# Every step of an attention-plus-MLP kernel listed one by one, with a new order for its first two batches

## The chip, the cores and the metric

The kernel runs on one core of a Trainium2 chip. The metric is the device time of one execution in microseconds (us). The engines are named as in the profile: PE (TensorE), DVE (VectorE), ACT (ScalarE), POOL (GpSimd) and SP (SyncE, which issues all transfers here); PEld is PE's weight loading. A measurement of this kernel tells about 0.3% from no change.

## What is computed

Eight batches of 8 heads, 576 tokens, head width 64, with 32 packed queries `p` per head; then a feed-forward layer over all 4608 tokens, 512 wide inside the model and 2048 wide in the middle:

```python
def sm_attn(qq, kk, vv):
    s = scale * np.matmul(qq, kk.transpose(0, 1, 3, 2))
    s = s - np.max(s, axis=-1, keepdims=True)
    a = np.exp(s)
    a = a / (np.sum(a, axis=-1, keepdims=True) + 1e-09)
    return np.matmul(a, vv)
p_packed = sm_attn(p, k, v)
out = sm_attn(q, p_packed, p_packed)
x = out.transpose(0, 2, 1, 3).reshape(B * S, H * D)
h = x @ w_in
g = h * (1.0 / (1.0 + np.exp(-1.702 * h)))
result = g @ w_out
```

## The kernel before

Inputs come as float32, except that the two weight matrices come as 64-bit floats, which the kernel turns into float32 itself. A weight piece is 128 rows of 512 numbers; there are 32, in `queue`: per chunk c of the 2048 middle columns four pieces of `w_in` ("in") and four of `w_out` ("out"). Piece n takes these steps: `load_w` (SP), `begin_w` (ACT: exponent scaled), `shift_w`, `sign_w`, `low_w` (DVE). An "out" piece is then split in a rounded upper part (`upper_w`, ACT) and the rest (`lower_w`, DVE, or two products on PE and an ACT copy for pieces 4 and 5). Raw pieces lie in 16 buffers that "in" and "out" pieces of a chunk share, so an "out" piece can be loaded only when an "in" piece has gone through `low_w`.

Attention of batch b, first pass: `scores1` (PE, in two halves of 288 tokens), maxima (DVE, `mx`), exponentials (ACT, `exp1`), `turn1` (transposes on PE, copies on ACT), `pack` (PE), `pack_end` (ACT), `pack_turn` (PE, then ACT): this gives `PT`. `m_chunk` multiplies `PT` with a chunk of `w_in`, so that the second attention pass and the first product of the feed-forward layer become one; its result is split in `mhi` (ACT) and `mlo` (DVE, `m_lower`). Second pass, per half: `scores2` (PE), `scores2_turn`, maximum and `sub2` (DVE), `exp2` (ACT), `sum2`, normalising and a transpose to `xt` (DVE), then a split in `ahi` (ACT) and `alo` (POOL, or PE and ACT in batch 0).

The feed-forward layer works in units (b, f): f is one of 16 pieces of 128 middle columns. `unit_h` gives six products `h` per half (upper and lower parts), tanh (ACT, `g`), the gate (DVE, `g` and, for the last 64 tokens, `over`), and a split in `ghi` (ACT) and `glo` (POOL). `unit_out` adds 3 products for each of four blocks of 128 tokens into `acc0` to `acc3`. The 64 tokens of a batch that are left over are done for two batches at once (`acc_over`). Batches 0 and 1 are interleaved, since weights are still being made: batch 0 chunk 0, batch 1 chunks 0 and 1, batch 0 chunks 1 to 3, batch 1 chunks 2 and 3; unfinished sums go to memory (`aside`) and come back (`back`).

Order: PE and SP execute in the order of the code. For DVE, ACT and POOL a scheduler with a model of times chose the order. The code is a hand-written list `lead` up to the first units, then a plan per unit. `warm(n)` is n products without use, which keep PE busy. The functions that the change touches:

Of the kernel before, what the change touches and what calls it, by code (L numbers as in the profile page):

```python
# [18 lines left out]
def kernel(  # L19
# [34 lines left out]
    P = 128  # L54
# [68 lines left out]
    def load(what, b, halves=(0, 1)):  # L123
        if what == "p":
            t = wk.tile([P, NP, NPK], F32, tag="p_sb", name=f"p_{b}", bufs=2)
            nc.sync.dma_start(t, pT[b])
            kq["p", b] = t
            return
# [8 lines left out]
        if what == "v":  # L137
            nc.sync.dma_start(
                t[:, : KC - 1, :], v[b, : (KC - 1) * P, :].rearrange("(c p) e -> p c e", p=P)
            )  # L140
            nc.sync.dma_start(t[:KLAST, KC - 1, :], v[b, (KC - 1) * P :, :])
        else:
            src = kT if what == "k" else qT
            for half in halves:
                nc.sync.dma_start(t[:, :, tokens(half)], src[b, :, :, tokens(half)])
# [50 lines left out]
    def low_w(n):  # L196

# [7 lines left out]
        if w[0] == "in" and w[1] > 0:  # L205
            load_w(("out", i))
# [10 lines left out]
    def lower_w_pe(n, bank):  # L217

        w = wo[slot_of(queue[n])]
        bank = bank(f"pswl_{n}")  # L220
        nc.tensor.matmul(bank, ident, dec[n], start=True, stop=False)
        nc.tensor.matmul(bank, minus, w[:, 0, :], start=False, stop=True)
        nc.scalar.copy(w[:, 1, :], bank)

    def make_w(*ns):


        for step in (begin_w, shift_w, sign_w, low_w):
# [26 lines left out]
    def scores1_first(eo, half):  # L255
# [7 lines left out]
        for j in range(NP):  # L263
            mm1(0, eo, half, bank, j)
        nc.vector.tensor_reduce(
            st["mx", 1, 0, eo][:, half : half + 1], bank[:, :NH], axis=AX.X, op=ALU.max
        )
        st["bank", eo, half] = bank

    def scores1(b, half):  # L270
# [3 lines left out]
        banks = [bank_b(f"ps1_{b}_{eo}_{half}") for eo in range(2)]  # L274
# [3 lines left out]
        for eo in range(2):  # L278
            nc.scalar.copy(st["x", 1, b, eo][:, tokens(half)], banks[eo][:, :NH])
            nc.vector.tensor_reduce(  # L280
                st["mx", 1, b, eo][:, half : half + 1], banks[eo][:, :NH], axis=AX.X, op=ALU.max
            )

    def exp1(b, eo):
        key = (1, b, eo)
        mx, x = st["mx", *key], st["x", *key]
        nb = wk.tile([P, 1], F32, tag="nb1", name=f"nb1_{b}_{eo}", bufs=2)
        st["sum", *key] = sm = wk.tile([P, 2], F32, tag="sm1", name=f"sm1_{b}_{eo}", bufs=2)
        nc.vector.tensor_scalar(nb, mx[:, 0:1], mx[:, 1:2], -SCALE, op0=ALU.max, op1=ALU.mult)
        if b > 0:  # L290
            nc.scalar.activation(x, x, AF.Exp, bias=nb, scale=SCALE, accum_out=sm[:, 0:1])
            return
        for half in range(2):
            nc.scalar.activation(
                x[:, tokens(half)], st["bank", eo, half][:, :NH], AF.Exp, bias=nb,
                scale=SCALE, accum_out=sm[:, half : half + 1],
            )
# [58 lines left out]
    def pack_turn(b):  # L356
        bank = bank_b(f"pspt_{b}")
        nc.tensor.transpose(bank[:, :P], st["P", b].rearrange("p e d -> p (e d)"), ident)
        st["PT", b] = PT = wk.tile([P, NP, NPK], F32, tag="PT", name=f"PT_{b}", bufs=3)
        nc.scalar.copy(PT.rearrange("p j n -> p (j n)"), bank[:, :P])  # L360

    def m_chunk(b, fc):

        PT = st["PT", b]
        banks = [bank_b(f"psm_{b}_{fc}_{eo}") for eo in range(2)]
        for j in range(NP):
            for eo in range(2):
# [6 lines left out]
                )  # L374
        for eo in range(2):
            hi = wk.tile([P, FC], F32R, tag=f"mhi{eo}", name=f"mhi_{b}_{fc}_{eo}", bufs=2)
            nc.scalar.copy(hi, banks[eo])  # L377
            st["m", b, fc, eo] = [hi, banks[eo]]

    def m_lower(b, fc):  # L380
        for eo in range(2):
            hi, bank = m = st["m", b, fc, eo]
            m[1] = wk.tile([P, FC], F32R, tag=f"mlo{eo}", name=f"mlo_{b}_{fc}_{eo}", bufs=2)
            nc.vector.tensor_tensor(m[1], bank, hi.bitcast(F32), op=ALU.subtract)  # L384
# [21 lines left out]
    def scores2_turn(b, half):  # L406
        x = st["x", 2, b, half]
        for eo, bank in enumerate(st["bank", 2, b, half]):
            nc.vector.transpose(x[:, eo * NH : (eo + 1) * NH], bank[:, :NH])
# [30 lines left out]
    def norm2(b, half):  # L440
        key = (2, b, half)
        x, rs = st["x", *key], st["rs", *key]
        st["t", *key] = t = x_tile(f"xt_{b}_{half}")
        nc.vector.tensor_tensor(groups(x), groups(x), over(rs), op=ALU.mult)
        nc.vector.transpose(t, x)
# [8 lines left out]
    def a_lower_pe(b, half, banks):  # L454
# [282 lines left out]
```

## Time and profile before

| | |
|---|---|
| time, median of 3 | 750.83 us (749.62 to 751.96) |
| profiled execution: time, span | 750.82 us, 748.7 us |
| mean granted clock of PE | 0.983 |
| busy: PE, DVE, ACT, POOL | 716.1, 345.9, 338.4, 239.3 us |
| moved by DMA | 60.08 MB, mean 80 GB/s |

Busy is the sum of the time in which an engine had an instruction in work. A list by stretches of time says in which stage an engine is full. In the chain of work that ended last each piece is followed back to what released it. A row of the timeline gives start, length, engine, line and, in brackets, the idle time before it and who ended it.

### The profile page before, as it was taken

The page shows a single profiled execution, that of the slowest core. Times are in us where ns is not written, and L with a number is a line of the kernel's source. Part 1 is how long each engine was busy: PE and PEld are TensorE (multiplying, and loading weights), DVE is VectorE, ACT ScalarE, POOL GpSimd, SP SyncE. Part 2 cuts the span into 40 slices and gives each one's busy share as a digit, 9 for nine tenths or more (in the row PEclk, how much of TensorE's full clock was granted, in tenths as well). Part 3 has the DMA queues.
Part 4 walks back from the last instruction along what each step waited for, and adds up shares of the span by engine and source line. Part 5 has one row for each costly group of instructions (what it writes and reads, how often), then busy time and mean ns, then how long its engine had stood idle before and what let it go on. Part 6 is the DMA issues. An engine that isn't in the chain of part 4 may idle for free.

```text
span 748.7 us, 13113 instructions
## 1 busy us (share of the span) xinstructions
PE 716.1 (96%) x5084; PEld 569.6 (76%) x5084; DVE 345.9 (46%) x808; ACT 338.4 (45%) x813; POOL 239.3 (32%) x292
## 2 busy tenths in 40 slices
PE   5687989999999999999999999999999999999997
PEld 4455877678877877878877888878887887888886
DVE  3789499953283227232274217243255226432220
ACT  3473566654344444353435434454335444443331
POOL 0022343343352324333343333423334323433332
PEclk7799999999999999999999999999999999999999
DMA  9750743640423021030213022021113100010002
GB/s 296 252 177 1 282 168 113 222 141 28 154 69 121 12 65 65 1 123 1 64 64 120 18 65 64 1 73 52 51 63 121 29 1 2 1 57 1 1 1 70
DMA packets 35133, 60.08 MB, mean 80 GB/s; under 512 B 2304, under 2 KB 19712, under 8 KB 35072
## 3 DMA queue, kind: packets, MB, share of 16 engines
q1 hardware_dynamic: 35072, 59.25, 23.8%
q8 instruction: 40, 0.66, 0.4%
q14 instruction: 21, 0.17, 0.1%
HBM read 47.71 MB, written 11.53 MB: 79 GB/s over the span
## 4 chain that ended last, share of the span: by engine, by line
PE 84%; DVE 10%; DMA 2%; ACT 1%; issue 1%; POOL 0%; SPq 0%; ACTq 0%; DVEq 0%
PE acc L528 43%; PE h L504 25%; PE acc_over L528 6%; PE psm L368 4%; DVE dec L191 2%; DMA raw<-w_in 2%; PE pspv L341 2%; PE ps L397 1%; PE ps L243 1%; DVE g L494 1%; DVE dec L187 1%; PE pst L317 1%; DVE dec L201 1%; DVE mlo L384 1%; DVE w_in L201 1%
## 5 line engine op out<-in xcount | busy, mean ns | idle before, releaser
L491 POOL TENSOR_TENSOR glo<-g,ghi 128x224 fp32r<-128x224 f32 (+1 forms) x256 | 198.2, 791 | 459.1 <-ACT ghi L490 458.6
L528 PE MATMUL acc<-wo,ghi 128*128 128x512 f32 x1024 | 320.9, 395 | 0.5 <-ACT ghi L490 0.5
L528 PEld LDWEIGHTS acc<-wo,ghi 128*128 128x128 f32 x1024 | 186.5, 189 | 36.7 <-ACT ghi_over L490 2.5
L494 DVE SCALAR_TENSOR_TENSOR g<-g,h 128x224 f32<-128x224 f32 (+1 forms) x256 | 105.5, 418 | 225.9 <-ACT g L509 225.3
L528 PE MATMUL acc<-wo,glo 128*128 128x512 f32 x512 | 201.9, 394 | 0.0
L509 ACT ACTIVATE g<-h 128x288 f32<-128x288 f32 x256 | 104.5, 411 | 161.2 <-PE h L504 157.0
L504 PE MATMUL h<-ahi,mhi 128*128 128x288 f32 x512 | 151.6, 311 | 6.5 <-DVE g L494 4.5
L504 PE MATMUL h<-ahi,mlo 128*128 128x288 f32 x512 | 144.3, 297 | 1.9 <-DVE mlo L384 1.8
L504 PEld LDWEIGHTS h<-ahi,mhi 128*128 128x128 f32 x512 | 96.6, 189 | 46.3 <-issue 28.8
L528 PEld LDWEIGHTS acc<-wo,glo 128*128 128x128 f32 x512 | 96.7, 189 | 22.9 <-POOL glo L491 0.6
L490 ACT CAST ghi<-g 128x224 fp32r<-128x224 f32 (+1 forms) x256 | 100.3, 402 | 23.7 <-DVE g L494 12.6
L504 PE MATMUL h<-alo,mhi 128*128 128x288 f32 x512 | 108.4, 293 | 0.0
L504 PEld LDWEIGHTS h<-ahi,mlo 128*128 128x128 f32 x512 | 96.8, 189 | 4.4 <-DVE mlo L384 2.3
L504 PEld LDWEIGHTS h<-alo,mhi 128*128 128x128 f32 x512 | 82.7, 188 | 0.0
L384 DVE TENSOR_TENSOR mlo<-psm,mhi 128x512 fp32r<-128x512 f32 x64 | 41.4, 685 | 74.6 <-ACT mhi L377 74.6
L377 ACT CAST mhi<-psm 128x512 fp32r<-128x512 f32 x64 | 34.3, 588 | 52.5 <-PE psm L368 52.5
L528 PE MATMUL acc_over<-wo,ghi_over 128*128 128x512 f32 x128 | 40.1, 395 | 0.5 <-ACT ghi_over L490 0.5
L368 PE MATMUL psm<-w_in,PT 64*32 64x512 f32 x512 | 36.9, 601 | 2.0 <-DVE w_in L201 2.0
L183 ACT ACTIVATE dec<-raw 128x512 f32<-128x512 f32 x32 | 21.4, 674 | 16.3 <-DMA raw<-w_in 9.0
L528 PEld LDWEIGHTS acc_over<-wo,ghi_over 128*128 128x128 f32 x128 | 23.4, 188 | 6.8 <-ACT ghi_over L490 1.4
L466 POOL TENSOR_TENSOR alo<-xt,ahi 128x576 fp32r<-128x576 f32 x14 | 20.0, 1429 | 23.1 <-ACT ahi L451 19.1
L494 DVE SCALAR_TENSOR_TENSOR over<-g,h 128x64 f32<-128x64 f32 x128 | 27.3, 213 | 0.0
(73 smaller groups left out, 482.1 us busy)
## 6 DMA issues: line engine op xcount, KB each, us to landing
k<-kT SPq DMA_DIRECT2D x16, 576.0 KB, 5.2
q<-qT SPq DMA_DIRECT2D x16, 576.0 KB, 5.4
raw<-w_in SPq DMA_DIRECT2D x16, 512.0 KB, 8.0
v<-v SPq DMA_DIRECT2D x8, 1024.0 KB, 5.8
raw<-w_out SPq DMA_DIRECT2D x16, 512.0 KB, 5.3
o<-o SPq DMA_DIRECT2D x24, 256.0 KB, 2.1
aside<-o SPq DMA_DIRECT2D x8, 256.0 KB, 2.1
back<-aside SPq DMA_DIRECT2D x8, 256.0 KB, 6.3
```

The source lines that it names most:

```text
L183: nc.scalar.activation(dec[n], upper, AF.Abs, scale=DOWN)
L191: nc.vector.scalar_tensor_tensor(t, raw[slot_of(queue[n])][:, :, 1], 0x80000000, t, op0=ALU.bitwise_and, op1=ALU.bitwise_or,)
L368: nc.tensor.matmul(banks[eo][32 * j : 32 * j + 32, :], PT[rows(eo), j, :], w_in_sb[fc][rows(eo), j, :], start=True, stop=True,)
L377: nc.scalar.copy(hi, banks[eo])
L384: nc.vector.tensor_tensor(m[1], bank, hi.bitcast(F32), op=ALU.subtract)
L466: nc.gpsimd.tensor_tensor(lo, st["t", 2, b, half], hi.bitcast(F32), op=ALU.subtract)
L490: nc.scalar.copy(hi, src)
L491: nc.gpsimd.tensor_tensor(lo, src, hi.bitcast(F32), op=ALU.subtract)
L494: nc.vector.scalar_tensor_tensor(dst, th, 1.0, h, op0=ALU.add, op1=ALU.mult)
L504: nc.tensor.matmul(h[:, :NH], m[eo][part][:, fo : fo + P], a[:, eo * NH : (eo + 1) * NH], start=(n == 0), stop=(n == len(terms) - 1),)
L509: nc.scalar.activation(g, h[:, :NH], AF.Tanh, scale=1.702)
L528: nc.tensor.matmul(acc, gp[:, at : at + P], wo[f][:, part, :], start=(start and i == 0), stop=(stop and i == 2),)
```

## The change

1. Every step that used two engines is split in functions for one engine each: for instance `scores1` into `scores1_mm` (PE), `scores1_copy` (ACT) and `scores1_max` (DVE), `unit_h` into `h_mm`, `h_tanh`, `h_gate`, `h_over`, `h_upper`, `h_lower`, `unit_out` into `out_mm`, `out_take` and `store`.
2. The whole program is one tuple `order` of such steps, and the scheduler is switched off for all engines: each executes its steps as they are listed.
3. For batches 0 and 1, and what runs beside them, the list is in a new order. From the first units of batch 2 on PE's order is the old one.

Each engine executes the same instructions as before; three further functions (`m_again`, `m_again_copy`, `h_lower_mm`) are defined and not used.

```diff
-    def scores1(b, half):
+    def scores1_mm(b, half):
...
-        for eo in range(2):
-            nc.scalar.copy(st["x", 1, b, eo][:, tokens(half)], banks[eo][:, :NH])
-            nc.vector.tensor_reduce(
-                st["mx", 1, b, eo][:, half : half + 1], banks[eo][:, :NH], axis=AX.X, op=ALU.max
-            )
+    def scores1_copy(b, half, eo):
+        bank = st["bank", 1, b, half][eo]
+        nc.scalar.copy(st["x", 1, b, eo][:, tokens(half)], bank[:, :NH])
+
+    def scores1_max(b, half, eo):
+        bank = st["bank", 1, b, half][eo]
+        nc.vector.tensor_reduce(
+            st["mx", 1, b, eo][:, half : half + 1], bank[:, :NH], axis=AX.X, op=ALU.max
+        )
...
+    order = (
+        (load, "k", 0, 0), (load_p, 0), (scores1_first, 1, 0), (scores1_first, 0, 0),
+        (max1_first, 0, 0), (load, "k", 0, 1), (scores1_first, 0, 1), (max1_first, 0, 1),
+        (bias1, 0, 0), (exp1_first, 0, 0), (scores1_first, 1, 1), (max1_first, 1, 1),
+        (max1_first, 1, 0), (exp1_first, 0, 1), (bias1, 0, 1), (exp1_first, 1, 0), (sum1, 0, 0),
+        (exp1_first, 1, 1), (sum1, 0, 1), (turn1_mm, 0, 0), (load_w, 1), (begin_w, 1),
+        (shift_w, 1), (turn1_last_mm, 0), (turn1_last_copy, 0), (warm, 4), (turn1_copy, 0, 0),
+        (sign_w, 1), (load_w, 0), (begin_w, 0), (load, "v", 0, 0), (turn1_mm, 0, 1),
+        (turn1_copy, 0, 1), (load, "v", 0, 1), (pack, 0), (warm, 8), (shift_w, 0), (sign_w, 0),
+        (low_w, 0), (low_w, 1), (load_w, 2), (begin_w, 2), (shift_w, 2), (sign_w, 2), (low_w, 2),
+        (pack_end, 0), (pack_turn_mm, 0), (pack_turn_copy, 0), (load, "q", 0, 0),
...
     )
-    b2 = [bank_acc(2), bank_acc(3)]
-    lead = (
-        (warm, 13), (scores1_first, 0, 0), (scores1_first, 0, 1), (scores1_first, 1, 0),
...
-    for step, *args in loads:
+    for step, *args in order:
         step(*args)
...
-    with tile.TileContext(nc) as tc, tc.manual_schedule(engines={mybir.EngineType.PE, mybir.EngineType.SP}):
+    with tile.TileContext(nc) as tc, tc.manual_schedule():
```

Three places in the order of instructions (a row: line, operation, what is written from what, size; times or waits are not in it). First DVE at the start of the program: `dec` and `w_in` are the decoding of weights, `mx` the maxima of the first scores `ps`, `nb` the bias for the exponential. Before:

```order
1 L187 TENSOR_SCALAR dec<-dec 128x512
2 L191 SCALAR_TENSOR_TENSOR dec<-raw_92,dec 128x512
3 L187 TENSOR_SCALAR dec<-dec 128x512
4 L201 SCALAR_TENSOR_TENSOR w_in_81<-raw_92,dec 128x512
5 L191 SCALAR_TENSOR_TENSOR dec<-raw_94,dec 128x512
6 L201 SCALAR_TENSOR_TENSOR w_in_81<-raw_94,dec 128x512
7 L265 TENSOR_REDUCE mx_0_0_125<-ps_0_0_0_126 128x1
8 L265 TENSOR_REDUCE mx_0_0_125<-ps_0_0_1_132 128x1
```

Now:

```order
1 L254 TENSOR_REDUCE mx_0_0_99<-ps_0_0_0_100 128x1
2 L254 TENSOR_REDUCE mx_0_0_99<-ps_0_0_1_107 128x1
3 L282 TENSOR_SCALAR nb_0_0_113<-mx_0_0_99 128x1
4 L254 TENSOR_REDUCE mx_0_1_92<-ps_0_1_1_117 128x1
5 L254 TENSOR_REDUCE mx_0_1_92<-ps_0_1_0_93 128x1
6 L282 TENSOR_SCALAR nb_0_1_125<-mx_0_1_92 128x1
7 L306 TENSOR_SCALAR sm_0_0_115<-sm_0_0_115 128x1
```

The two weights, which stood ahead of the maxima, now come behind all of the first softmax. On PE at the same place `warm` are the products without use, `pst` and `pstl` the transposes of `turn1`, `pspv` is `pack`. Before:

```order
1 L114 MATMUL warm<-ident 128x128 x13
2 L243 MATMUL ps_0_0_0_126<-k_89,p_85 32x288 x4
3 L243 MATMUL ps_0_0_1_132<-k_89,p_85 32x288 x4
4 L243 MATMUL ps_0_1_0_140<-k_89,p_85 32x288 x4
5 L243 MATMUL ps_0_1_1_146<-k_89,p_85 32x288 x4
6 L317 MATMUL pst_0_165<-ident,x_0_0_124 128x128 x4
7 L317 MATMUL pst_1_176<-ident,x_0_1_138 128x128 x4
8 L323 MATMUL pstl_182<-ident,x_0_0_124 64x128
9 L323 MATMUL pstl_182<-ident,x_0_1_138 64x128
10 L114 MATMUL warm<-ident 128x128 x4
11 L341 MATMUL pspv_201<-v_96,aT_164 32x64 x40
```

Now:

```order
1 L229 MATMUL ps_0_1_0_93<-k_87,p_89 32x288 x4
2 L229 MATMUL ps_0_0_0_100<-k_87,p_89 32x288 x4
3 L229 MATMUL ps_0_0_1_107<-k_87,p_89 32x288 x4
4 L229 MATMUL ps_0_1_1_117<-k_87,p_89 32x288 x4
5 L317 MATMUL pst_0_139<-ident,x_0_0_98 128x128 x4
6 L328 MATMUL pstl_149<-ident,x_0_0_98 64x128
7 L328 MATMUL pstl_149<-ident,x_0_1_91 64x128
8 L114 MATMUL warm<-ident 128x128 x4
9 L317 MATMUL pst_1_166<-ident,x_0_1_91 128x128 x4
10 L348 MATMUL pspv_173<-v_164,aT_138 32x64 x40
11 L114 MATMUL warm<-ident 128x128 x8
```

The 13 warm-up products have left the start (they now stand behind the first `m_chunk`), and 8 of them moved from behind `scores2` to behind `pack`. Last SP, behind the loads of batch 0: `k`, `v`, `q` are batch 1's, `raw` are weight pieces. Before:

```order
13 L145 DMA k_242<-kT 128x4x288 x2
14 L169 DMA raw_245<-w_out 128x1024
15 L138 DMA v_280<-v 128x4x512
16 L141 DMA v_280<-v 64x512
17 L169 DMA raw_283<-w_out 128x1024
18 L169 DMA raw_389<-w_out 128x1024
19 L145 DMA q_433<-qT 128x4x288 x2
20 L169 DMA raw_436<-w_in 128x1024
```

Now:

```order
15 L141 DMA k_337<-kT 128x4x288
16 L171 DMA raw_380<-w_out 128x1024
17 L141 DMA k_337<-kT 128x4x288
18 L171 DMA raw_424<-w_out 128x1024
19 L171 DMA raw_439<-w_in 128x1024
20 L143 DMA v_448<-v 128x4x512
21 L171 DMA raw_473<-w_in 128x1024
22 L171 DMA raw_483<-w_in 128x1024
23 L147 DMA v_448<-v 64x512
```

Three "in" pieces (9, 8 and 24) now stand ahead of batch 1's `q`; before, the first of them came behind it.

More of the change, by code (lines that the diff above doesn't have):

```diff
@@ L121, with load_p, load @@
     kq = {}
[L123 to L128, printed above, removed]
+    def load_p(b):
+        t = wk.tile([P, NP, NPK], F32, tag="p_sb", name=f"p_{b}", bufs=2)
+        nc.sync.dma_start(t, pT[b])
+        kq["p", b] = t
+    def load(what, b, part):
         if (what, b) not in kq:
@@ L452, in a_upper, with a_lower_mm @@
         st["a", b, half] = (hi, lo)
[L454 removed]
+    def a_lower_mm(b, half, banks):
         hi, lo = st["a", b, half]
@@ L577, in over_out, with over_take, over_store @@
             product(accs[0], g, f, n * P, f == 0, f == NF - 1)
[L578 to L583 removed]
+    def over_take(pair):
+        taken["over"] = o_tile(f"o_over_{pair}")
+        nc.scalar.copy(taken["over"], accs[0])
+    def over_store(pair, k):
+        at = (2 * pair + k + 1) * S - REST
+        nc.sync.dma_start(out[at : at + REST, :], taken["over"][k * REST : (k + 1) * REST, :])
@@ L648 @@
-    for entry in first:
-        put(*entry)
-    for u, b, c in chunks[3:]:
-        put(u - 5, m_step, b, c)
-    for b in range(2):
-        put(at(b, NF - 1) - 4, back, b)
-    for n in range(2, B):
-        u = at(n, 0)
-        for what in "pkv":
-            put(u - 21, load, what, n)
-        put(u - 19, scores1, n, 0)
-        put(u - 18, scores1, n, 1)
-        put(u - 17, load, "q", n)
-        for eo in range(2):
-            w = u - 18 + 2 * eo
-            put(w, exp1, n, eo)
-            put(w + 1, sum1, n, eo)
-            put(w + 4, turn1, n, eo)
-        put(u - 11, pack, n)
-        put(u - 11, pack_end, n)
-        put(u - 10, pack_turn, n)
-        for half in range(2):
-            w = u - 8 + half
-            put(w, scores2, n, half)
-            put(w, sub2, n, half)
-            put(w, exp2, n, half)
-            put(w + 1, sum2, n, half)
-            put(w + 1, turn2, n, half)
@@ L677 @@
-    load("p", 0)
-    table(AF.Exp)
-    for step, *args in loads:
-        step(*args)
-    for step, *args in lead:
-        step(*args)
-    def ready(u):
-        if u[0] == "over":
-            over_h(*u[1:])
-        else:
-            for half in range(2):
-                unit_h(*u[:2], half)
-    ahead = 6
-    for i, u in enumerate(units[CF:], CF):
-        for step, args in plan[i]:
-            step(*args)
-        while ahead < len(units) and ahead - 2 <= i:
-            ready(units[ahead])
-            ahead += 1
-        if u[0] == "over":
-            over_out(*u[1:])
-        else:
-            unit_out(*u)
+    ends = {}
```

1048 lines of the change are left out of this document (849 added, 199 removed).

## The prediction

> **What bounds the kernel now.** I read the page first, then busy time by stretches of 20 us, then the chain that ended last, then the timeline of the first 40 us.
>
> ```profile
> span 748.7 us, 13113 instructions
> PE 716.1 (96%) x5084; PEld 569.6 (76%) x5084; DVE 345.9 (46%) x808; ACT 338.4 (45%) x813; POOL 239.3 (32%) x292
> ```
>
> By stretches, the columns after the length are PE, PEld, DVE, ACT and POOL busy, the granted clock, the DMA share and GB/s:
>
> ```profile
> 0.00:20.00 20.00, 11.59 (x80) 9.41 (x84) 6.90 (x20) 6.95 (x17) 0.70 (x6) 0.76 0.91 303
> 20.00:40.00 20.00, 13.70 (x183) 9.03 (x182) 15.87 (x32) 9.08 (x20) 0.26 (x1) 0.82 0.62 210
> 40.00:60.00 20.00, 15.88 (x168) 10.53 (x167) 17.41 (x39) 13.70 (x33) 4.29 (x5) 0.95 0.48 165
> 60.00:80.00 20.00, 16.63 (x97) 12.33 (x97) 14.71 (x28) 8.54 (x18) 6.57 (x7) 0.88 0.04 14
> 80.00:100.00 20.00, 19.58 (x133) 15.49 (x132) 13.49 (x28) 12.20 (x28) 6.56 (x8) 1.00 0.95 355
> 100.00:120.00 20.00, 17.18 (x101) 13.47 (x100) 19.22 (x38) 11.87 (x27) 9.15 (x8) 1.00 0.31 106
> 120.00:140.00 20.00, 18.77 (x106) 14.76 (x104) 20.00 (x39) 12.36 (x28) 6.82 (x8) 1.00 0.32 113
> 160.00:180.00 20.00, 20.00 (x122) 16.64 (x121) 5.89 (x18) 8.78 (x23) 6.92 (x10) 1.00 0.15 43
> ```
>
> From 160 us on PE is full (20.00 of 20.00) and nothing but less PE work could help. Before that PE has holes, at a clock below 1 up to 80 us, while DVE is the fuller engine from 20 to 60 us and again, entirely full, from 100 to 140 us.
>
> ```profile
> 144.94 1.20 DVE mlo L384 x2
> 146.14 0.37 DVE g L494
> 146.55 1.83 PE h L504 x12
> ...
> 238.20 2.75 PE acc_over L528 x12
> ...
> 302.91 2.78 PE acc L528 x12
> 307.25 2.78 PE acc L528 x12
> ...
> 410.60 2.75 PE acc_over L528 x12
> ```
>
> In the chain (start, length, what) DVE work leads nearly without a break from 88 us to 146.5 us, and PE leads from there to the end. So the time is set by when PE becomes full, and in the last part of the ramp DVE sets that.
>
> **What the change can touch.** By the order of instructions, every engine has the same instructions as before, none added and none taken away; only their places change, and on PE these are the same again from the last group into acc_over of the first pair of batches on: 238.20 us here. That part I put at a change of 0. All that counts is when PE gets to that group.
>
> How late is PE there? One pair later the same group stands at 410.60, so a pair is worth 172.4 us of PE. The first pair has besides to do the head of batches 2 and 3, and the splits that run on PE, about 16.5 us (an estimate, from the warm pieces of scores, chunks, packs and two units of h in the same chain). So 189 us of full-speed work end at 238.2: PE is **49 us** late. In the same terms DVE was idle 32.4 us up to 140 us (140 less the sum of seven DVE columns, 107.6) and about 33.5 us at 146.5. The other 15.5 us are how far DVE's work ran ahead of PE's at the last wait on it.
>
> **Part 1: the head, up to the first h.**
>
> ```profile
> 1.36 5.76 PE L114 MATMUL warm<-ident 128*128 128x128 f32 x26 [1.36 <-POOL ident masks.py:199]
> 7.05 1.64 PE L243 MATMUL ps<-k,p 64*32 64x288 f32 x32
> 10.13 0.43 DVE L187 TENSOR_SCALAR dec<-dec 128x512 uint32<-128x512 uint32 x1 [10.13 <-ACT dec L183]
> 13.69 1.18 DVE L265 TENSOR_REDUCE mx<-ps 128x1 f32<-128x288 f32 x3
> 15.09 0.50 ACT L294 ACTIVATE x<-ps,nb 128x288 f32<-128x288 f32 x1 [3.71 <-DVE nb L289]
> 24.36 2.05 PE L114 MATMUL warm<-ident 128*128 128x128 f32 x16
> 32.49 0.77 DVE L445 STREAM_TRANSPOSE xt<-x 128x576 f32<-128x576 f32 x1
> 36.30 0.45 PE L504 MATMUL h<-ahi,mhi 128*128 128x288 f32 x1
> ```
>
> The scores are done at 8.7 us, but DVE's order puts the decoding of two weights, which wait for their transfer, ahead of the maxima: these start at 13.69, five microseconds late. Now the maxima stand first. k's first half is now the first transfer; the old start at 7.05 came just as 13 warm-up matmuls ended, so it can be a little earlier, but with the warm-up gone the scores run at a slow clock. I set one against the other: scores done near 8.7, two maxima and a bias 1 us (449 ns each by 1.18 for three that overlap), first exponential near 9: **6 us earlier**.
>
> From the first exponential to the first h took 36.30 - 15.09 = 21.2 us. What changes on that way: warm 8 moves from beside the softmax to between pack and its transpose, and ACT's begin_w of weight 2 stands ahead of pack_end: together about 1.5 us more (2.05 for the eight, part of it beside the wait for the weight). Weight 3 and q's second half now follow v, weight 2 and q's first half: 5.7 MB are listed up to there, and the first row moved 303 GB/s x 20 us = 6.1 MB, so they land by 19 to 20 us, just in time for DVE (turns, max, sub come first). DVE's stretch from the turn of the scores to the transposed exponentials takes 9 us as before, and the last split runs with a warm PE (13 warm-ups beside DVE's work), about 1 us less. So 21 us again: first h near 30 us, xt ready near 28 us instead of 33.3, with one half of batch 1's scores done earlier. PE is 22 us late there instead of 29. The moved loads of w1, w0 cost nothing: ACT meets them only after the exponentials.
>
> **Part 2: from there to where PE is full.** I count the listed work in front of the tightest waits of PE on DVE, by these groups (busy in total, mean ns):
>
> ```profile
> L191 DVE SCALAR_TENSOR_TENSOR dec<-raw,dec 128x512 uint32<-128x512 uint32 x32 | 26.2, 828 | 0.2
> L187 DVE TENSOR_SCALAR dec<-dec 128x512 uint32<-128x512 uint32 x32 | 15.4, 496 | 15.4 <-ACT dec L183 15.3
> L201 DVE SCALAR_TENSOR_TENSOR dec<-raw,dec 128x512 uint32<-128x512 uint32 x16 | 12.3, 776 | 0.1
> L215 DVE TENSOR_TENSOR wo<-dec,wo 128x512 fp32r<-128x512 f32 x14 | 10.4, 752 | 0.7 <-ACT wo L211 0.7
> L494 DVE SCALAR_TENSOR_TENSOR g<-g,h 128x288 f32<-128x288 f32 x128 | 57.6, 450 | 199.6 <-ACT g L509 199.0
> L494 DVE SCALAR_TENSOR_TENSOR over<-g,h 128x64 f32<-128x64 f32 x128 | 27.3, 213 | 0.0
> L384 DVE TENSOR_TENSOR mlo<-psm,mhi 128x512 fp32r<-128x512 f32 x64 | 41.4, 685 | 74.6 <-ACT mhi L377 74.6
> L409 DVE STREAM_TRANSPOSE x<-ps 128x288 f32<-128x288 f32 x32 | 13.3, 453 | 17.5 <-PE ps L397 17.5
> L425 DVE TENSOR_TENSOR x<-x,mx 128x576 f32<-128x576 f32 x16 | 13.7, 856 | 0.0
> L436 DVE TENSOR_REDUCE sm<-x 128x18 f32<-128x576 f32 x16 | 12.0, 750 | 4.6 <-ACT x L429 4.6
> L444 DVE TENSOR_TENSOR x<-x,rs 128x576 f32<-128x576 f32 x16 | 15.0, 940 | 0.4
> ```
>
> All DVE groups add up to 382 us against 345.9 busy, since neighbours overlap, so I scale sums by 0.905. Up to xt of batch 0 the new list holds four weights (8.3 us), a softmax half (4.9), three turns (1.4), two m_lower (1.4) and the first maxima, biases and sums (2.8): 18.7 x 0.905 = 16.9. At 28 us DVE has then idled 11.5 us; before it was 16.8 (33.3 less 6.9 of the first row and 9.6 of the second's 15.87).
>
> The chunk m_chunk(0, 2) waits for low_w of weight 18. Ahead of it DVE has 21 shifts, 20 signs, 20 lows, 6 lowers (46.7 us), 26 gates (10.9, at a mean of 0.418 over both widths), 12 overs (2.6), four softmax halves with their eight turns (22), 8 m_lower (5.5) and small steps (7): 95 x 0.905 = 85.7 us. PE has ahead of it 27 h and 45 products; a unit of two h and four products has a period of 4.34 us (302.91 to 307.25), so 0.79 and 0.69 each: 21.3 + 31.1, and 19.3 for scores, chunks, packs and turns: 71.7. The distance is 14.0 us. It is 14.4 at the first h of batch 1 and stays between 11 and 14 for all waits between them; it is not one late step but DVE's total. Thus PE is at least 14 + 11.5 = 25.5 us late, plus the idle time d that DVE still gathers over these 69 us of its work.
>
> This d is what no row shows, since the order is new. With none: gain 49 - 25.5 = 23.5 us. With all of the old one, 33.5 - 16.8 = 16.7 us: gain 6.8. By the share of time, the old DVE idled 15% from 33 to 146 us, which gives 12 us here; in its fullest stretch, 100 to 140, 2%, which gives 1.4. I take **10**, near the first of these, because the new order puts ACT and DVE steps of the same thread close together in fixed order and each handover shows as a hole. Gain 13.5 us. PE waits that are not DVE's (POOL's low parts of g, stores, SP's order) I take at nothing: SP is free to run ahead, loads of weights 8, 9 and 24 now go out in the stretch where 0.04 of DMA was used; without that cover a transfer costs 5 us once.
>
> **Sum.** The profiled execution took 750.8 us (748.7 of span), the median is the same. 750.8 - 13.5 = **737 us**.
>
> **The clock.** PE restarts at 15.7 us and gets its clock back some 4.5 us later:
>
> ```profile
> 18.00:20.00 2.00, 2.00 (x14) 1.77 (x16) 0.60 (x2) 1.33 (x3) 0.00 (x0) 0.50 1.05 418
> 20.00:22.00 2.00, 1.90 (x81) 1.46 (x80) 1.21 (x2) 0.04 (x1) 0.00 (x0) 0.88 0.36 124
> ```
>
> The Trainium skill (TensorE: Matmul & The Clock Gate, What's actually happening) says the clock is half until about 3.4 us of sustained activity and falls back after an idle window. By that rule, which these rows bear out, taking away the first warm-up is no saving in itself.
>
> **Rivals.** *The clock stays at half through the head* (chance 0.08): no window of PE is long enough before the first h. Then warm 8, the transpose, one half of the scores, the chunk and the split take twice as long, about 4 us on the path: 741. Against it: from turn1 through pack PE has 6 us of work in one piece.
> *Only the head gains* (0.16): d is as before, 16.7 us, lost in handovers: 750.8 - 6.8 = 744. For it: DVE idled 5 to 6.5 us per 20 between 60 and 100 us.
> *DVE is nearly full* (0.10): d under 3 us, 728 to 730.
> *ACT stands behind weights* (0.08, slower):
>
> ```profile
> ACT dec L183 <- DMA raw<-w_in: 9.0, 3, 7.0
> ```
>
> ```profile
> raw<-w_out SPq DMA_DIRECT2D x16, 512.0 KB, 5.3
> ```
>
> (Above: us in total, times, longest; below: median us from issue to landing.) Twelve output weights use the buffers that input weights of their chunk leave, and begin_w now has a fixed place on ACT, for weight 12 directly behind its load. Where it comes before the transfer, all tanh steps behind it wait up to 5.3 us, and DVE and PE with them. From three such waits on (13.5 / 5.3) the gain is gone; with five, 750.8 - 13.5 + 26.5 = 764. Against it: the list leaves 6 to 9 us of DVE work between the release and most begin_w.
> *Handovers eat all of it* (0.04): d of 23, no change.
>
> My forecast (730 to 741) has 0.54. Faster: 0.54 + 0.08 + 0.10 and 0.14 of the second: 0.86; within 0.3% (2.3 us, what a measurement of this kernel tells apart): 0.06; slower: 0.08. The range 728 to 750 leaves out the slow case and the best of the full-DVE one.
>
> **What the next profile would show.** First exponential near 9 us and first h near 30; acc_over's last group of the first pair near 225 instead of 238; DVE above 90% from 30 to 110 us; PE full from about 110 us. Wrong would be: waits of ACT on raw of more than 5 us in sum, or holes of PE after 120 us.

## The result, and the profile after

| | before | after |
|---|---|---|
| median of the runs taken together | 751.39 us (749.62 to 751.99) | 729.25 us (728.5 to 729.89) |
| profiled execution: time, span | 750.82, 748.7 us | 728.5, 726.7 us |
| mean granted clock of PE | 0.983 | 0.998 |

The changed kernel is faster: the ratio of the times is 0.9709, with a 95% interval of 0.9689 to 0.9729. A second comparison gave 0.9718 (0.9704 to 0.9733). The gain is 22 us; 13.5 were forecast, with 737 us in a range of 728 to 750. The time lies inside that range, 1.25 us above its lower end.

The first lines of the page after, span and busy time of the engines:

```profile
span 726.7 us, 13097 instructions
...
PE 708.6 (98%) x5084; PEld 564.0 (78%) x5084; DVE 347.0 (48%) x808; ACT 335.0 (46%) x813; POOL 236.1 (32%) x292
```

PE's matmuls are the same in number, and busy for 7.5 us less (716.1 before); its idle time fell from 32.6 to 18.1 us, by 14.5. Together that is the whole 22.0 us of span. The stretches after, with the columns as before (length, busy PE, PEld, DVE, ACT, POOL, granted clock, DMA share, GB/s):

```profile
0.00:20.00 20.00, 10.73 (x163) 6.92 (x163) 8.61 (x22) 7.97 (x21) 0.70 (x6) 1.00 0.90 291
20.00:40.00 20.00, 17.15 (x142) 11.64 (x142) 19.50 (x42) 13.55 (x31) 1.61 (x2) 1.00 1.05 368
40.00:60.00 20.00, 19.16 (x205) 13.62 (x204) 18.94 (x39) 12.11 (x29) 6.50 (x7) 1.00 0.44 155
60.00:80.00 20.00, 19.95 (x117) 15.77 (x117) 19.36 (x37) 12.40 (x28) 9.58 (x9) 1.00 0.58 195
80.00:100.00 20.00, 19.96 (x128) 16.09 (x134) 18.89 (x37) 12.38 (x31) 8.01 (x9) 1.00 0.53 184
100.00:120.00 20.00, 19.65 (x138) 14.72 (x122) 17.52 (x35) 12.38 (x29) 8.20 (x10) 1.00 0.44 145
120.00:140.00 20.00, 20.00 (x141) 16.32 (x134) 14.24 (x32) 12.33 (x31) 6.42 (x8) 1.00 0.62 208
```

PE is nearly full from 40 us on, not from 160, and from 40 to 100 us DVE is nearly full beside it. The recorded clock is 1.00 throughout (for the first 20 us that has to be read with care, see the last section), so the matmuls that were stretched before, at 0.82 to 0.95 of the clock from 20 to 80 us, are short now. The chain that ended last goes over PE and DVE in turn up to 59.45 us, is PE from there to 106 us, goes once more over ACT, DVE and POOL up to 116 us, and is PE from there to the end. Its rows also give the places on which the prediction rested (start, length, what):

```profile
49.15 0.83 DVE x L437 x2
...
59.45 0.66 PE h L533 x3
...
99.73 1.12 PE psm L377 x16
...
106.30 0.41 ACT g L541
...
115.98 0.50 PE acc L594
...
212.21 5.54 PE acc_over L594 x24
...
387.69 2.76 PE acc_over L594 x12
...
560.36 2.77 PE acc_over L594 x12
```

The row at 99.73 is `m_chunk(0, 2)`. The row at 212.21 holds the last two groups into `acc_over` of the first pair; the last of them starts halfway, at 214.98, where it stood at 238.20: 23.2 us earlier. The next pair's group stands at 387.69 instead of 410.60 (22.9), and the end of the span is 22.0 earlier. The gain is made ahead of 215 us; one us of it is lost again behind.

In the head (start, length, engine, line, what; in brackets the idle time before and who ended it):

```profile
8.23 1.22 PE L229 MATMUL ps<-k,p 64*32 64x288 f32 x16 [1.36 <-DMA k<-kT]
10.29 0.50 ACT L291 ACTIVATE x<-ps,nb 128x288 f32<-128x288 f32 x1 [7.86 <-DVE nb L282]
27.06 0.76 DVE L475 STREAM_TRANSPOSE xt<-x 128x576 f32<-128x576 f32 x1
29.90 0.29 PE L533 MATMUL h<-ahi,mhi 128*128 128x288 f32 x1
```

First exponential 4.8 us earlier, `xt` ready at 27.8 instead of 33.3, first h 6.4 us earlier. PE's waits on other engines from 36 to 220 us are these two, against 12.6 us in the twelve largest kinds before (us in total, times, longest):

```profile
PE h L533 <- DVE mlo L417: 0.8, 1, 0.8
PE acc L594 <- POOL glo L520: 0.3, 1, 0.3
```

The way from the first h to the end of the last group into `acc_over`, before and then after (columns as in the stretches):

```profile
36.30:240.95 204.65, 191.18 (x1341) 147.07 (x1341) 140.91 (x297) 109.25 (x254) 71.82 (x76) 0.98 0.39 134
29.90:217.75 187.85, 186.15 (x1326) 144.60 (x1325) 143.35 (x300) 106.66 (x254) 68.83 (x76) 1.00 0.44 150
```

So 6.4 us of the 23.2 are gained ahead of the first h and 16.8 behind it. Of these 16.8, PE's idle time gives 11.8 (13.5 before, 1.7 now) and its shorter busy time 5.0.

### The profile page after: what moved, and what is told of

It reads as the page before. It is cut to its first block, busy times and chain, and to the rows that moved or that the text cites. A ratio compares the mean times of both kernels' runs of the same rounds, so it can differ in the third digit from the quotient of the medians.

```text
span 726.7 us, 13097 instructions
## 1 busy us (share of the span) xinstructions
PE 708.6 (98%) x5084; PEld 564.0 (78%) x5084; DVE 347.0 (48%) x808; ACT 335.0 (46%) x813; POOL 236.1 (32%) x292
## 4 chain that ended last, share of the span: by engine, by line
PE 93%; DVE 3%; DMA 1%; ACT 1%; issue 1%; POOL 0%; SPq 0%; ACTq 0%
PE acc L594 47%; PE h L533 29%; PE acc_over L594 6%; PE psm L377 4%; PE pspv L348 2%; PE ps L426 1%; PE ps L229 1%; PE pst L317 1%; DMA k<-kT 1%; PE warm L114 1%; DVE sm L464 0%; DVE mlo L417 0%; DVE x L453 0%; DVE sm L465 0%; ACT x L291 0%
## 5 line engine op out<-in xcount | busy, mean ns | idle before, releaser
L520 POOL TENSOR_TENSOR glo<-g,ghi 128x288 fp32r<-128x288 f32 (+1 forms) x256 | 195.1, 778 | 442.4 <-ACT ghi L564 438.3
L594 PEld LDWEIGHTS acc<-wo,ghi 128*128 128x128 f32 x1024 | 184.2, 188 | 44.1 <-issue 7.3
L523 DVE SCALAR_TENSOR_TENSOR g<-g,h 128x288 f32<-128x288 f32 (+1 forms) x256 | 106.0, 417 | 218.1 <-ACT g L541 217.7
L533 PE MATMUL h<-ahi,mhi 128*128 128x288 f32 x512 | 149.4, 307 | 0.1
L564 ACT CAST ghi<-g 128x288 fp32r<-128x288 f32 (+1 forms) x256 | 100.3, 403 | 32.0 <-DVE g L523 16.5
L520 POOL TENSOR_TENSOR glo_over<-over,ghi_over 128x512 fp32r<-128x512 f32 x16 | 20.6, 1293 | 16.8 <-ACT ghi_over L584 16.8
```

The lines of the kernel that those rows point to most:

```text
L520: engine.tensor_tensor(lo, src, hi.bitcast(F32), op=ALU.subtract)
L523: nc.vector.scalar_tensor_tensor(dst, th, 1.0, h, op0=ALU.add, op1=ALU.mult)
L533: nc.tensor.matmul(h[:, :NH], m[eo][part][:, fo : fo + P], a[:, eo * NH : (eo + 1) * NH], start=(n == 0), stop=(n == len(terms) - 1),)
L564: nc.scalar.copy(g_tiles((b, f))[0][:, half * NH : half * NH + src.shape[1]], src)
L594: nc.tensor.matmul(acc, gp[:, at : at + P], wo[f][:, part, :], start=(start and i == 0), stop=(stop and i == 2),)
```

## The experiments

Three theories were written down beforehand. A: the time is set by DVE, by the idle time that it gathers until PE is full, about 5 us of it in the head. B: it is PE's clock, which no longer falls to half. C: the scheduler's order of DVE, ACT and POOL was bad, and any order listed by hand gives the gain. All ratios are to the kernel before, in the same comparison. "Against the changed kernel" means against 0.9714, the mean of its two ratios, times 750.8 us; such a difference is uncertain by about 2 us.

**1. The old code with the scheduler off for all engines** (DVE, ACT and POOL in the order of the code):

```diff
-    with tile.TileContext(nc) as tc, tc.manual_schedule(engines={mybir.EngineType.PE, mybir.EngineType.SP}):
+    with tile.TileContext(nc) as tc, tc.manual_schedule():
```

> The kernel before, with the scheduler off for ACT, DVE and POOL too: these follow the code's old order, in which the first maxima stand ahead of the weights. Theory A (what counts is how long DVE idles until PE is full: 33.5 us before, about 15 us after; 5 us of the difference lie ahead of the first exponential): the head's 5 us are gained, the middle stays as it was or loses, 742 to 750. Theory B (the gain is PE's clock, which fell to half four times before and never after): no gain unless the clock holds, about 750. Theory C (the gain is that the scheduler's order on DVE and ACT is gone): most of the 22 us, about 730.

Measured: 813.04 us, ratio 1.0846 (1.0813 to 1.0878), 63 us slower than before. Stretches of this run, and PE's waits from 36 to 220 us:

```profile
40.00:60.00 20.00, 17.49 (x185) 13.07 (x185) 9.17 (x22) 10.43 (x25) 2.21 (x3) 0.95 0.35 127
60.00:80.00 20.00, 13.47 (x71) 10.49 (x69) 14.56 (x29) 8.15 (x19) 6.54 (x7) 0.83 0.03 12
80.00:100.00 20.00, 15.41 (x70) 10.61 (x71) 11.57 (x26) 8.51 (x19) 4.27 (x6) 0.83 0.94 333
```

```profile
PE h L504 <- DVE g L494: 10.7, 7, 3.0
PE psm L368 <- DVE w_in L201: 7.7, 2, 4.3
PE h L504 <- ACT mhi L377: 6.2, 1, 6.2
```

DVE is busy 9.17 to 14.56 of 20 us, where the scheduler kept it at 13.49 to 17.41. C falls: a list is not good because it is a list. The figures of A (742 to 750) and B (about 750) for this run were missed too: steps that are written as a block for several engines leave each engine waiting for the others (PE for DVE's gate and for weights, DVE for 13.1 us in all for ACT's scaled weights).

**2. The new code with the scheduler on again for DVE, ACT and POOL** (PE and SP as listed):

```diff
-    with tile.TileContext(nc) as tc, tc.manual_schedule():
+    with tile.TileContext(nc) as tc, tc.manual_schedule(engines={mybir.EngineType.PE, mybir.EngineType.SP}):
```

> The changed kernel with the scheduler on again for ACT, DVE and POOL; PE and SP keep the new list. A: the first maxima still stand first, so the head's 5 us stay; DVE's order in the middle is another, with some more holes: 730 to 738. B: PE's order and its warm-ups are the new ones, so the clock holds: 729. C: the scheduler's order takes back most of the gain: 745 to 751.

Measured: 739.21 us, ratio 0.9853 (0.9825 to 0.9881): about 10 us slower than the changed kernel. The same stretches, first of the changed kernel, then of this one:

```profile
36.00:100.00 64.00, 63.07 (x468) 48.93 (x476) 61.19 (x122) 40.25 (x96) 24.89 (x26) 1.00 0.55 188
100.00:180.00 80.00, 79.65 (x605) 62.61 (x590) 56.96 (x123) 44.55 (x108) 25.50 (x32) 1.00 0.43 142
```

```profile
36.00:100.00 64.00, 58.29 (x427) 43.55 (x428) 63.85 (x127) 41.42 (x94) 22.97 (x23) 1.00 0.54 189
100.00:180.00 80.00, 75.99 (x555) 59.52 (x553) 51.63 (x107) 40.14 (x99) 24.95 (x30) 1.00 0.28 97
```

Under the scheduler DVE is fuller (63.85 of 64 us against 61.19), and still PE does 4.8 us less in that stretch and 3.7 less in the next. PE now waits for DVE's gate (us in total, times, longest; 36 to 220 us):

```profile
PE h L533 <- DVE over L523: 4.3, 4, 1.6
PE h L533 <- DVE g L523: 2.1, 3, 1.5
```

A's figure, 730 to 738, was missed by 1 us, those of B (729) and C (745 to 751) by more. A in its simple form falls: it is not enough that DVE is never idle, it must also do first what PE needs next. B does not explain these 10 us: the clock reads 1.00 in both stretches, and they are missing all the same.

**3 and 4. The scheduler on for ACT and POOL alone, and for DVE alone:**

```diff
-    with tile.TileContext(nc) as tc, tc.manual_schedule():
+    with tile.TileContext(nc) as tc, tc.manual_schedule(engines={mybir.EngineType.PE, mybir.EngineType.SP, mybir.EngineType.DVE}):
```

> The changed kernel with the scheduler on for ACT and POOL alone; DVE, PE and SP keep the new list. With the scheduler on for all three the time was 739.2, although DVE idled no more than in the changed kernel. If DVE's order is what counts (which of its steps come first): 729 to 731. If the orders of ACT and POOL count: 736 to 740.

> The other half: the scheduler on for DVE alone; ACT, POOL, PE and SP keep the new list. If DVE's order is what counts: 737 to 741, or more where ACT in fixed order now waits for a DVE step that comes later. If those of ACT and POOL count: 729 to 732.

Measured: 733.46 us, ratio 0.9764 (0.9748 to 0.9781), with DVE listed; 733.18 us, ratio 0.9761 (0.9747 to 0.9776), with ACT and POOL listed (the second one's edit names `Activation` and `Pool` in place of `DVE`). One row for each, from 36 to 180 us, DVE listed first:

```profile
36.00:180.00 144.00, 139.32 (x1028) 108.10 (x1029) 119.54 (x240) 85.13 (x199) 49.89 (x57) 1.00 0.45 150
```

```profile
36.00:180.00 144.00, 139.56 (x1028) 107.86 (x1028) 114.69 (x236) 81.70 (x197) 47.88 (x56) 1.00 0.44 151
```

Both times lie between the figures expected for the two answers (729 to 732 and 736 to 741). Each half of the list costs 3.5 to 4 us when it is handed to the scheduler, both together 10. PE's busy time in this window tells the same: 142.72 us in the changed kernel (the two rows above added), 139.3 and 139.6 here, 134.28 in run 2. The order of ACT and POOL is worth as much as that of DVE, although in this window ACT is busy 59% and POOL 35% of the time in the changed kernel.

**5. Two weights loaded and decoded ahead of the first maxima again**, as they were before the change:

```diff
-        (load, "k", 0, 0), (load_p, 0), (scores1_first, 1, 0), (scores1_first, 0, 0),
-        (max1_first, 0, 0), (load, "k", 0, 1), (scores1_first, 0, 1), (max1_first, 0, 1),
+        (load, "k", 0, 0), (load_p, 0), (load, "k", 0, 1), (load_w, 1), (load_w, 0),
+        (begin_w, 1), (shift_w, 1), (sign_w, 1), (begin_w, 0), (shift_w, 0), (low_w, 1),
+        (sign_w, 0), (low_w, 0), (scores1_first, 1, 0), (scores1_first, 0, 0), (max1_first, 0, 0), (scores1_first, 0, 1), (max1_first, 0, 1),
...
```

(Left out: the same ten steps are taken from their later places.)

> The changed kernel with weights 1 and 0 decoded ahead of the first maxima on DVE and ACT, as it was before the change; all else is the new list. A: the first exponential comes about 4 us later (near 14 instead of 10.3), but the 2.5 us of decoding that now stand there are gone later, so DVE has idled 2 to 4 us more: 731 to 734. B: PE idles longer than 3 us there and its clock is half for longer, but it is so in the changed kernel's first 15 us too: 729 to 732. C: 729.

Measured: 734.49 us, ratio 0.9794 (0.977 to 0.9819): 6 us slower than the changed kernel, where A expected 731 to 734, B 729 to 732 and C 729. The first exponential starts at 15.21 (15.09 before the change), `xt` at 31.95, and the first h at 36.39 (36.30 before). Putting the maxima first is worth about 6 us, near the prediction's head term (16.8 less 11.5 us of idle DVE). The run moves the transfers of the two weights as well, so it prices the two together.

**6 and 7. Twelve needless subtractions on DVE** (`pad`, 128x512, as a rule 0.68 us each), between listed steps 110 and 385, and between 640 and 915:

```diff
+    def pad():
+        nc.vector.tensor_tensor(pad_out, w_in_sb[0][:, 0, :], w_in_sb[0][:, 1, :], op=ALU.subtract)
...
+        (pad,), (h_lower, 0, 1, 0), (load_w, 24), (h_gate, 0, 1, 1), (sign_w, 6), (h_tanh, 0, 0,
...
```

> The changed kernel with 12 more DVE instructions, a subtraction of two 128x512 tiles into a scratch tile that nobody reads, one at every 25th step from step 110 to 385 (about 35 to 90 us); each costs some 0.61 us, 7.3 in all. A: DVE is 96% busy there, so nearly all of it reaches the end: 735 to 737. B and C: DVE is not what counts: 729 to 730.

> The same 12 subtractions on DVE as in the run with pads in the ramp, but at every 25th step from step 640 to 915 (about 125 to 195 us), where DVE is 54 to 72% busy and PE full. A: nothing, 729 to 730. If instead any DVE work in this part counts (through the gates, which PE waits for): up to 736.

Measured: 736.1 us, ratio 0.9811 (0.9786 to 0.9837), with the pads from 35 to 96 us: 7.3 us slower than the changed kernel. With the pads from 136 to 199 us: 730.77 us, ratio 0.9738 (0.9718 to 0.9759), 1.8 us slower, which the intervals hardly part from none. The profiled executions part them: from the first h to the start of the last two `acc_over` groups the changed kernel takes 182.3 us (table at run 12), the run with late pads 184.3, the one with early pads 190.0. The run with early pads, from 36 to 100 us, and PE's longest waits there:

```profile
36.00:100.00 64.00, 59.01 (x424) 43.79 (x424) 61.50 (x122) 36.83 (x87) 22.29 (x23) 0.97 0.53 181
```

```profile
PE ps L426 <- DVE x L437: 1.6, 1, 1.6
PE h L533 <- DVE over L523: 1.3, 3, 0.7
```

Twelve times 0.68 us, scaled by 0.905 for overlap as in the prediction, is 7.4 us: every us of DVE work added in the ramp is a us of time, and behind it about a quarter (2 of 8 us), where A expected nothing. A's main point holds: in the ramp DVE has no slack, though PE shows only 1 us of waits in the changed kernel.

**8. Fourteen subtractions less on DVE in the ramp** (`lower_w` given to POOL):

```diff
-        nc.vector.tensor_tensor(w[:, 1, :], dec[n], w[:, 0, :].bitcast(F32), op=ALU.subtract)
+        nc.gpsimd.tensor_tensor(w[:, 1, :], dec[n], w[:, 0, :].bitcast(F32), op=ALU.subtract)
```

> The changed kernel with the 14 lower parts of output weights (lower_w) made on POOL instead of DVE: 14 x 0.62 = 8.7 us less for DVE, about 14 x 1.3 = 18 us more for POOL, which is idle for 60% there. If DVE alone is the bound of the ramp, as A in its simple form has it: 722 to 724. If PE, which is 99% busy from 40 us on, is as much a bound: at most the 1.2 us of its holes after 40 us, 728 to 729. If POOL's queue then holds back the lower parts of g: 731 or more.

Measured: 732.96 us, ratio 0.9769 (0.975 to 0.9788): 4 us slower than the changed kernel. POOL takes 1425 ns for each, DVE took about 690. PE's waits, 36 to 220 us:

```profile
PE acc L594 <- POOL wo L211: 2.2, 3, 1.3
PE acc L594 <- POOL glo L520: 1.8, 4, 0.9
```

This is the third case of the forecast (731 or more): PE now waits 4.0 us for POOL. DVE does not save all that was taken from it either: fourteen times 0.69 is 9.7 us, and from 36 to 180 us it is busy 6.0 us less (112.27, against 118.31 in the second execution of the changed kernel, run 12); that fits what the last section shows of DVE beside POOL. So this way of relieving DVE costs more than it brings. Whether less work on DVE would gain anything without more on POOL was not tried. PE is idle only 1.7 us between the first h and the end of the `acc_over` groups in the changed kernel, so, as an estimate from that number, no more than this is left to gain there.

**9 to 11. The head again:** no warm-up products at all; `p` as the first transfer; and `p` first, thirteen warm-ups ahead of the scores, none behind, `pack_end` ahead of `begin_w` of weight 2.

```diff
-        (shift_w, 1), (turn1_last_mm, 0), (turn1_last_copy, 0), (warm, 4), (turn1_copy, 0, 0),
+        (shift_w, 1), (turn1_last_mm, 0), (turn1_last_copy, 0), (turn1_copy, 0, 0),
...
```

(Left out: `(warm, 8)` and `(warm, 13)` are taken out in the same way.)

```diff
-        (load, "k", 0, 0), (load_p, 0), (scores1_first, 1, 0), (scores1_first, 0, 0),
-        (max1_first, 0, 0), (load, "k", 0, 1), (scores1_first, 0, 1), (max1_first, 0, 1),
+        (load_p, 0), (load, "k", 0, 0), (load, "k", 0, 1), (scores1_first, 1, 0), (scores1_first, 0, 0),
+        (max1_first, 0, 0), (scores1_first, 0, 1), (max1_first, 0, 1),
```

```diff
-        (load, "k", 0, 0), (load_p, 0), (scores1_first, 1, 0), (scores1_first, 0, 0),
-        (max1_first, 0, 0), (load, "k", 0, 1), (scores1_first, 0, 1), (max1_first, 0, 1),
+        (warm, 13), (load_p, 0), (load, "k", 0, 0), (load, "k", 0, 1), (scores1_first, 1, 0), (scores1_first, 0, 0),
+        (max1_first, 0, 0), (scores1_first, 0, 1), (max1_first, 0, 1),
...
-        (low_w, 0), (low_w, 1), (load_w, 2), (begin_w, 2), (shift_w, 2), (sign_w, 2), (low_w, 2),
-        (pack_end, 0), (pack_turn_mm, 0), (pack_turn_copy, 0), (load, "q", 0, 0),
+        (low_w, 0), (low_w, 1), (load_w, 2),
+        (pack_end, 0), (pack_turn_mm, 0), (pack_turn_copy, 0), (begin_w, 2), (shift_w, 2), (sign_w, 2), (low_w, 2), (load, "q", 0, 0),
```

> The changed kernel without any of the 25 warm-up products (4 behind the first transposes, 8 behind pack, 13 behind the first chunk). A: 4 and 8 lie in the chain that ended last (1.7 and 2.0 us), but q's second half lands only at 22.4 us and DVE is busy from 20 us on, so at most 1.5 us are gained: 728 to 729. B: without them PE's clock is half until it has been busy for a while: through pack, scores, chunk and the first h, PE work of about 8 us takes twice as long, and the ramp is later by 3 to 8: 732 to 737.

> The changed kernel with the transfer of p ahead of both halves of k, as before the change. k's second half, for which PE waits until 8.22 us, then is issued about 0.3 us earlier and landed by 7.5 us before the change: the first exponential comes 0.5 to 0.7 us earlier. A: all of it reaches the end through DVE: 728.5. If the rest of the head is tied to the transfers of q and weight 3 (22.4 us), which stay: 729.2.

> A shorter head: p ahead of k (in the run with that alone the first exponential came 1.1 us earlier, and all of it was lost at a slow pack and at warm-ups), the 13 warm-ups at the start back, those of 4 and 8 gone, and pack_end ahead of weight 2 on ACT. Pack then ends near 16.2 and the second scores start near 17.3 instead of 19.0. If the head's DVE chain sets the end: 1 to 1.5 us less than the changed kernel, ratio near 0.969. If the transfers of q's second half and weight 3 set it (21 to 22.4 us): the same as the changed kernel, 0.971.

Measured: 729.23 us, ratio 0.9718 (0.97 to 0.9736); 728.33 us, ratio 0.9705 (0.9687 to 0.9723); 730.59 us, ratio 0.9726 (0.971 to 0.9741). None of the three can be told from the changed kernel, nor can run 10 decide between its two expected figures (728.5 and 729.2). With `p` first the first exponential starts at 9.21, and in the third at 8.61, 1 to 1.7 us earlier, but then `pack` waits for `v` and the second scores for `q`. The third run's rows:

```profile
14.28 2.83 PE L348 MATMUL pspv<-v,aT 128*32 128x64 f32 x80 [1.72 <-DMA v<-v]
...
20.80 1.21 PE L426 MATMUL ps<-q,PT 64*32 64x288 f32 x16 [1.01 <-DMA q<-qT]
```

From 10 us on the transfers lead the head: an earlier start ends at the same `v` and `q`. B's forecast for the run without warm-ups, 732 to 737, is refuted; the recorded clock did fall there (0.91 from 20 to 40 us), and the time did not move by more than the runs can tell.

**12. The changed kernel once more**, in the last comparison:

> The changed kernel once more, on the same chip and beside the same runs of the kernel before as the shorter head: 729, ratio 0.971.

Measured: 729.88 us, ratio 0.9718 (0.9704 to 0.9733). Its profiled execution differs from the first in the head, which makes it useful: with the runs on the head it shows what a late head costs. Starts in us, profiled executions:

| run | first `xt` | first h | last two `acc_over` groups | from first h to these | span |
|---|---|---|---|---|---|
| changed kernel | 27.06 | 29.90 | 212.21 | 182.31 | 726.7 |
| `p` first | 27.39 | 30.24 | 212.53 | 182.29 | 727.1 |
| no warm-ups | 28.12 | 31.82 | 213.88 | 182.06 | 728.4 |
| changed kernel again | 28.64 | 31.49 | 213.79 | 182.30 | 728.3 |
| `p` first, warm-ups ahead | 28.69 | 32.74 | 214.82 | 182.08 | 729.3 |
| weights first | 31.95 | 36.39 | 218.44 | 182.05 | 732.8 |

The two executions of the changed kernel are 1.58 us apart at `xt`, 1.59 at the first h and 1.58 at the groups. In all six the groups start 182.05 to 182.31 us behind the first h: a late first h is passed on one for one, and what lies behind it takes the same time. `xt` alone does not decide: in the run with `p` first and warm-ups ahead, `xt` comes as in the second execution of the changed kernel, but the first h comes 1.25 us later and the groups 1.03 later. The first h follows `xt` by 2.84 or 2.85 us in three of the six, and by 3.70 to 4.44 in the three whose recorded clock is below 1 from 28 to 36 us (0.79, 0.96 and 0.79, in the order of the table).

This distance also tells what the other runs cost behind the head: 192.6 us with the scheduler on for three engines (10.3 more), 186.7 with DVE listed and 186.0 with ACT and POOL listed, 186.7 with `lower_w` on POOL.

No version here beats the changed kernel by more than the measurements can tell.

## Why the prediction was right, and where it was off

The time lies inside the range, but below the 730 to 741 of the forecast itself, and the gain is 8.5 us larger than forecast. The places and the head were right; one term of the sum was three times too large, and two more were off by 2 and 5 us in ways that partly cancel.

**Place.** Right: the part of PE's order from the last `acc_over` group on took the same time (172.7 us from one pair to the next, 172.4 before), and all of the gain is made ahead of it.

**The head.** Right in size. Forecast: first h near 30, measured 29.90; `xt` ready near 28, measured 27.8; DVE idle by then 11.5 us, measured 11.5 (28 us less 16.47 busy); the forecast's own listed work gives 11.1 (28 less 16.9), so the last digits agree by luck. The split with a warm PE, put at about 1 us less, was that: from `xt` to the first h it took 3.81 us before and 2.84 now. The first exponential was put near 9 and came at 10.29: k's second half landed later than assumed (PE's row at 8.23 waits for it), and 16 scores took 1.22 us. Runs 10 and 11 speak for this having cost nothing, since `v` and `q` lead afterwards. The head's worth, 6.3 us forecast at the first h, is 6.4 there and about 6 by run 5.

**The term that was mis-sized is d,** the idle time that DVE still gathers in the ramp. Forecast 10, "near the first" of two bounds. Measured: DVE is busy 85.3 us up to 100 us (the first five stretches), so idle 14.7, of which 11.5 were there at 28: d is **3.2**. The rival "DVE is nearly full" (d under 3, 728 to 730 us), at a chance of 0.10, is nearest to what happened. The reason given for taking 10 was that each handover of ACT and DVE would show as a hole. It does not: the list mostly puts steps of other threads between, and from 36 to 100 us DVE is idle 2.8 us in all. The lower bound, 1.4 us from DVE's fullest stretch before, was the better guide here.

With 3.2 the prediction's own sum gives 49 - 14 - 11.5 - 3.2 = 20.3 us, 730.5 us of time. That it comes so near is in part luck, for PE's work was counted wrongly on both sides of `m_chunk(0, 2)`, which starts at 99.73. Between the first h and there PE is busy 68.5 us, for what was counted as 63.7 (71.7 less the 8 done at 30 us); from there to the last `acc_over` group it is busy 114.9 us for a counted 117.3 (189 less 71.7). So DVE's list was not 14.0 us longer than PE's, but about 9, and the 49 us that PE was said to be late were about 2 too many by this count. With all three mended, 46.6 - 9.2 - 11.5 - 3.2, the sum says 22.7 us; the group came 23.2 us earlier.

**Where PE becomes full.** Wrong: forecast 110 us, seen at 36 to 40. The prediction had DVE lead and PE wait all along the ramp; in the new list both are nearly full, and the chain goes over both.

**The other signs.** DVE above 90% from 30 to 110 us: up to 100 us (18.89 to 19.50 of 20 from 20 us on); from 100 to 110 us it is 85%. The last `acc_over` group near 225: 214.98, by the size of d. Waits of ACT on raw weights, the rival on the slower side:

```profile
ACT dec L182 <- DMA raw<-w_in: 1.7, 2, 1.0
```

1.7 us, far from the three waits of 5.3 that would have decided; none is for an output weight. No hole of PE after 120 us: the stretch from 120 to 140 is full. Rival "only the head gains": refuted by the ramp, which gave some 16 of the 22 us; 10 of these are the order on DVE, ACT and POOL (run 2); how the other 6 divide between PE's new order, the clock of the ramp and the rest was not tried apart. (PE's busy time behind the first h is 5.0 us shorter than before; 0.72 us of that is half of batch 1's scores, which now come ahead of the first h, and the fuller clock may be another part.) Rival "the clock stays at half": the scores at 19.01 took 0.72 us, as at 27.91, so PE was fast by then. In runs 9 and 11 they took 1.21 and 1.22, and the time stayed the same within 1 us, where this rival had put 4.

## What to carry to other kernels

Where one engine feeds another through a ramp, count the feeder's listed work ahead of each wait of the other, and look at the best stretch that the old schedule reached before taking its mean idle time: here the best stretch was nearer. An engine that is never idle can still be 10 us too late if it does the wrong things first: look at who waits, not at how full it is. To part a late head from a slow ramp, take the distance between two marks of the engine that should be full; it agreed within 0.3 us in six executions here. Listing by hand paid only with an order by need; the old code listed as it stood was 8% slower than with the scheduler.

## What was not expected of the hardware

**DVE beside POOL.** Some DVE instructions take longer while POOL works, others never. Rows of the changed kernel, POOL's first, then DVE's:

```profile
66.63 1.02 POOL L520 TENSOR_TENSOR glo<-g,ghi 128x288 fp32r<-128x288 f32 x1 [1.39 <-ACT ghi L564]
68.92 3.33 POOL L520 TENSOR_TENSOR glo<-g,ghi 128x224 fp32r<-128x224 f32 x3 [1.27 <-ACT ghi L564]
```

```profile
62.91 0.45 DVE L523 SCALAR_TENSOR_TENSOR g<-g,h 128x288 f32<-128x288 f32 x1 [0.32 <-ACT g L541]
...
66.31 0.68 DVE L190 SCALAR_TENSOR_TENSOR dec<-raw,dec 128x512 uint32<-128x512 uint32 x1
67.02 1.18 DVE L199 SCALAR_TENSOR_TENSOR w_in<-raw,dec 128x512 uint32<-128x512 uint32 x1
68.12 0.42 DVE L186 TENSOR_SCALAR dec<-dec 128x512 uint32<-128x512 uint32 x1
...
70.56 1.15 DVE L190 SCALAR_TENSOR_TENSOR dec<-raw,dec 128x512 uint32<-128x512 uint32 x1
```

The `dec` of L190 at 66.31 lies nearly all ahead of POOL's work or in its first part and takes 0.68 us, the one at 70.56 lies inside it and takes 1.15. Over the rows from 20 to 220 us that show one instruction each: L190 takes 0.67 to 0.69 us in all 17 cases without POOL, and 0.68 to 1.32, median 1.06, in the 11 that overlap POOL by 0.3 us or more (median 0.80 in run 12; some of the 11 are not slowed at all); the shift of L186 0.38 to 0.43 in 17, and 0.42 to 1.05, median 0.89, in 8. The gates, `mlo` and `back`, which read one operand that PE wrote, stay at their length in all 21 overlapping cases (at most 0.46 and 0.69), and so do transposes and sums (L464). A small instruction shows it best: the `sm` of L465, 128x18, takes 0.17 to 0.18 us in the three cases without POOL, and 0.56 to 0.97 in the three beside it. POOL's rows, then DVE's:

```profile
52.26 0.67 POOL L520 TENSOR_TENSOR glo<-g,ghi 128x224 fp32r<-128x224 f32 x1 [3.65 <-ACT ghi L564]
57.09 1.42 POOL L502 TENSOR_TENSOR alo<-xt,ahi 128x576 fp32r<-128x576 f32 x1 [0.94 <-ACT ahi L481]
```

```profile
52.27 0.69 DVE L465 TENSOR_SCALAR sm<-sm 128x18 f32<-128x18 f32 x1
57.58 0.97 DVE L465 TENSOR_SCALAR sm<-sm 128x18 f32<-128x18 f32 x1
```

Both times it ends 0.03 to 0.04 us behind POOL's instruction, as if it had waited for that one's end, and both lie on the chain that ended last: by the difference to 0.18 us, some 1.3 us of it. The Trainium skill (GPSIMD Engine Reference, Key points) says that GpSimd shares its SBUF interfaces with VectorE, with contention for DVE instructions that have two SBUF inputs or run in a 2-port mode. The slowed two-operand rows agree with it; that the one-operand instructions of L186 and L465 are hit would need the second case, and no row here names an instruction's mode. No run took POOL's work away, so this is a correlation in the traces, though a clean one.

**The recorded clock at the start.** It reads 1.00 from 0 to 20 us, while 16 scores took 1.22 us there (the row at 8.23) against 0.72 later:

```profile
27.91 0.72 PE L229 MATMUL ps<-k,p 64*32 64x288 f32 x16
```

In run 11, with 13 warm-ups ahead of them, the same 16 scores took 0.72 us at 6.07, and the recorded clock was 1.00 as well. So in these traces the recorded clock at the start of the program does not show how fast PE runs; the length of a known matmul does.
